# Attention and a gated feed-forward block: turning x by DMA, packing attention into the first half of the output stage, turning q in halves, and moving a set of value rims behind the weights

## The chip, the cores and the metric

The kernel runs on one core of a Trainium2 chip. The metric is the time of one execution on the device, in microseconds (us). Executions of one kernel mostly agree within a few tenths of a per cent (the kernel before: 277.99 to 278.3 us in four runs). Four engines do the work: PE (matrix products), DVE and ACT (vector and scalar work), POOL (here mostly copies and the issue of loads). SP here only issues DMA transfers (its timelines hold nothing else). In the views, PEld is the loading of PE's weights.

## The reference, cut to what matters

```python
# q, k, v: (4 batches, 8 heads, 768 positions, 64)
k_sum = k in blocks of 32 positions, maximum of each block
v_sum = v in blocks of 32 positions, mean of each block
scores = window of 16 positions on each side, and all 24 block sums (+ log 32)
attn   = softmax(scores) @ concat(v, v_sum)
x      = attn, heads side by side: (3072 tokens, 512)
out    = x + sigmoid(x @ w_res) * ((gelu(x @ w_gate) * (x @ w_val)) @ w_out)   # d_ff = 1536
```

## The kernel before: the parts that matter

The tokens are worked off in eight units of 384 (a batch is two units). Each unit has a projection stage (12 groups: a gate product `g` and a value product `vv` of four matmuls each, Gelu on ACT, their product `gvT` on DVE) and an output stage (three blocks of 128 tokens: `res_step` for the sigmoid, twelve matmuls `f` with w_out, the end on DVE). The attention of the *next* unit is woven into the output stage: per head pair scores `s` (PE), the exponential `P` (ACT), the mask (DVE), the product with v, `ao` (PE), and the normalized `xn` (DVE). The projection's matmuls are written for x with features on the partitions (`xT`), so `xn` is turned (transposed): on PE, by three transposes per feature block (0.17 us), and a copy by DVE (0.35 us).

```python
def xt_step(u, ko, st, pool, tag, copy=nc.vector.tensor_copy):
    xp = pool.tile([128, TU], BF16, tag=tag, name="xp")
    for sub in range(NSUB):
        nc.tensor.transpose(xp[:, sub * 128:(sub + 1) * 128],
                            st["xn"][:, sub, ko * 128:(ko + 1) * 128], ident[:])
    copy(st["xT"][:, ko, :], xp[:])

def mid_out(u, st, gvT, nst):              # output stages 1 to 6
    n = u + 1
    s_step(n, 0, nst)
    res_step(st, 0)
    ffn_step(st, gvT, 0, 0, FO)            # the 12 f matmuls of block 0
    av_step(n, 0, nst)
    s_step(n, 1, nst)
    end_step(u, st, 0)
    res_step(st, 1)
    ffn_step(st, gvT, 1, 0, 4)
    av_step(n, 1, nst)
    s_step(n, 2, nst)
    ffn_step(st, gvT, 1, 4, FO)
    av_step(n, 2, nst)
    s_step(n, 3, nst)
    xt_step(n, 0, nst, ps_t, "t")
    # ... av_step 3 and xt_step 1 to 3 among the f matmuls of block 2
```

The scores have one PSUM buffer (`ps_s`, bufs=1): the scores of the second head pair wait until the exponential of the first has read them. In units 3 and 5 DVE also makes the block maxima of k for the next batch (`k_blocks`, four times a reduction and a copy), after projection groups 4 to 7. The value rims (`v_rims`) are the 16 positions on each side of a window, which DMA copies from the neighbouring blocks of v.

The softmax here doesn't subtract the row's maximum and nothing guards it: scores larger than these inputs give would overflow.

## Time and profile before

The median is 278.05 us (277.99 to 278.26). PE is what bounds it. The first lines of the profile page, the kernel before (engine, busy us, share of the span, instructions), and two rows of its 40 slices (tenths of busy PE; tenths of the granted clock):

```profile
PE 262.2 (95%) x2352; PEld 142.7 (52%) x2377; DVE 161.9 (59%) x365; ACT 128.7 (47%) x204; POOL 101.2 (37%) x134
...
PE   6889989999999999999989999999899999999994
...
PEclk9999999999999999999999999999999999999999
```

The share says only that PE is busy nearly throughout. What a change can gain is read by stage. The windows view of the kernel before follows, with a window from the start of each stage to the start of the next. Columns: from and to; length; busy us of PE, PEld, DVE, ACT and POOL (instructions in brackets); granted clock; DMA share; GB/s. The six rows are output stage 0, output stage 1, projection 3, output stage 3, projection 4 and output stage 4.

```profile
41.61:56.24 14.63, 13.93 (x158) 6.87 (x158) 7.12 (x16) 8.16 (x12) 5.48 (x9) 1.00 1.42 174
76.89:90.72 13.83, 13.57 (x155) 7.05 (x158) 8.64 (x19) 7.81 (x9) 13.83 (x20) 1.00 1.41 106
122.04:140.74 18.70, 17.10 (x112) 9.42 (x110) 14.92 (x24) 5.93 (x13) 7.72 (x8) 1.00 0.24 43
140.74:154.57 13.83, 13.57 (x155) 7.05 (x158) 8.64 (x19) 7.81 (x9) 13.83 (x20) 1.00 1.68 123
154.57:170.48 15.91, 15.91 (x100) 9.29 (x98) 7.93 (x15) 5.93 (x13) 7.23 (x11) 1.00 1.65 189
170.48:184.31 13.83, 13.57 (x155) 7.04 (x158) 8.64 (x19) 7.81 (x9) 0.00 (x0) 1.00 0.09 34
```

A middle output stage takes 13.83 us every time. A plain projection stage takes 15.91 us, projection 3 takes 18.70. Its block sums (12 matmuls) explain 0.76 us; the other 2 us are mostly PE waiting for DVE (its busy time is 17.10 of the 18.70). The PE timeline of the kernel before shows the turning of x at the end of output stage 4 (start, length, instruction; a line merges several), and the waits of projection 3 in brackets, with what ended them:

```profile
136.52 0.81 PE L307 MATMUL g<-xT,w_gate 128*128 128x384 bf16 x4 [0.23 <-DVE gvT L313]
139.34 0.81 PE L307 MATMUL g<-xT,w_gate 128*128 128x384 bf16 x4 [1.37 <-DVE gvT L313]
...
183.97 0.50 PE L296 MATMUL xp<-ident,xn 128*128 128x128 bf16 x6
184.31 1.03 PE L307 MATMUL g<-xT,w_gate 128*128 128x384 bf16 x4
185.18 0.81 PE L307 MATMUL vv<-xT,w_val 128*128 128x384 bf16 x4
```

Six transposes hold PE from 183.97 to 184.31, so three cost 0.17 us and the twelve of a unit 0.68 us. The first group's `g` needs 0.87 us to the start of `vv` instead of 0.65: it waits for DVE's copies of the last two turned blocks (the second ends at 184.96, and the last matmul of `g` starts at 185.0).

The start is bound by DMA: it moves 196 to 208 GB/s in every 4 us from 24 to 44 us, PE waits 0.82 us for q until 36.15, and output stage 0 begins its f matmuls when w_out lands:

```profile
44.08 1.90 PE L339 MATMUL f<-w_out,gvT 128*128 128x512 bf16 x8 [0.29 <-DMA w_out<-in_moe_w_out_dram]
```

### The profile page before, as it was taken

The page shows a single profiled execution, that of the slowest core. Times are in us where ns is not written, and L with a number is a line of the kernel's source. Part 1 is how long each engine was busy: PE and PEld are TensorE (multiplying, and loading weights), DVE is VectorE, ACT ScalarE, POOL GpSimd, SP SyncE. Part 2 cuts the span into 40 slices and gives each one's busy share as a digit, 9 for nine tenths or more (in the row PEclk, how much of TensorE's full clock was granted, in tenths as well). Part 3 has the DMA queues.
Part 4 walks back from the last instruction along what each step waited for, and adds up shares of the span by engine and source line. Part 5 has one row for each costly group of instructions (what it writes and reads, how often), then busy time and mean ns, then how long its engine had stood idle before and what let it go on. Part 6 is the DMA issues. An engine that isn't in the chain of part 4 may idle for free.

```text
span 276.5 us, 5854 instructions
## 1 busy us (share of the span) xinstructions
PE 262.2 (95%) x2352; PEld 142.7 (52%) x2377; DVE 161.9 (59%) x365; ACT 128.7 (47%) x204; POOL 101.2 (37%) x134
## 2 busy tenths in 40 slices
PE   6889989999999999999989999999899999999994
PEld 2445644555545555446544565446444555555543
DVE  5856423598338533685947743685947743684424
ACT  1776347474565446343345336343256336343320
POOL 8795672340699932000799912000800000000000
PEclk9999999999999999999999999999999999999999
DMA  5999999999089999104099997104001100111003
GB/s 89 169 134 195 196 204 206 153 164 165 6 54 139 197 145 153 40 38 94 2 68 135 191 188 109 40 38 95 1 0 40 76 2 0 40 39 40 0 0 114
DMA packets 91274, 26.00 MB, mean 94 GB/s; under 512 B 75176, under 2 KB 88304, under 8 KB 91248
## 3 DMA queue, kind: packets, MB, share of 16 engines
q0 software_dynamic: 63664, 14.69, 57.9%
q1 hardware_dynamic: 27584, 10.96, 19.1%
q8 instruction: 18, 0.29, 0.4%
q14 instruction: 8, 0.07, 0.1%
HBM read 29.36 MB, written 6.29 MB: 129 GB/s over the span
## 4 chain that ended last, share of the span: by engine, by line
PE 75%; DMA 11%; DVE 4%; POOL 4%; issue 3%; ACT 1%; POOLq 0%; DVEq 0%
PE f L339 20%; PE g L307 19%; PE vv L307 18%; PE r L329 7%; DMA w_out<-in_moe_w_out_dram 5%; DMA w_gate<-in_moe_w_gate_dram 4%; PE ao L285 3%; PE s L267 3%; DMA q_sb<-in_q_dram 3%; PE xp L296 2%; DVE ks L199 2%; DVE gvT L313 2%; POOL vext L104 1%; PE f L360 1%; PE tp L224 1%
## 5 line engine op out<-in xcount | busy, mean ns | idle before, releaser
L313 DVE TENSOR_TENSOR gvT<-ge,vv 128x384 bf16<-128x384 f32 x96 | 52.6, 552 | 58.5 <-PE vv L307 56.4
L312 ACT ACTIVATE ge<-g 128x384 f32<-128x384 f32 x96 | 47.0, 491 | 82.7 <-DVE gvT L313 42.9
L307 PE MATMUL g<-xT,w_gate 128*128 128x384 bf16 x384 | 80.0, 326 | 2.5 <-DVE gvT L313 2.3
L307 PE MATMUL vv<-xT,w_val 128*128 128x384 bf16 x384 | 78.4, 326 | 0.3 <-DVE gvT L313 0.3
L339 PE MATMUL f<-w_out,gvT 128*128 128x512 bf16 x262 | 62.6, 379 | 1.6 <-issue 1.0
L307 PEld LDWEIGHTS <-w_val 128*128 128x128 bf16 x384 | 37.4, 98 | 26.3 <-issue 1.9
L307 PEld LDWEIGHTS <-w_gate 128*128 128x128 bf16 x384 | 35.7, 98 | 27.5 <-issue 5.8
L271 ACT ACTIVATE P<-s,bias_t 128x768 bf16<-128x768 f32 x32 | 28.9, 902 | 31.9 <-PE s L267 31.8
L257 POOL COPY vext<-vsum 32x1536 bf16<-32x1536 bf16 x14 | 20.0, 1467 | 62.9 <-DMA vsum<-vpart 62.8
L339 PEld LDWEIGHTS <-gvT 128*128 128x128 bf16 x276 | 26.1, 98 | 29.9 <-DMA w_out<-in_moe_w_out_dram 0.8
L104 POOL DMA_DIRECT2D vext<-in_v_dram x48 | 33.1, 761 | 13.3 <-DMA w_out<-in_moe_w_out_dram 5.3
L274 DVE TENSOR_TENSOR P<-P,maskt 128x768 bf16<-128x768 bf16 x32 | 17.7, 556 | 20.6 <-ACT P L271 18.9
L329 PE MATMUL r<-w_res,xT 128*128 128x512 bf16 x88 | 23.9, 381 | 0.4
L345 DVE SCALAR_TENSOR_TENSOR th<-th,f 128x512 f32<-128x512 f32 (+1 forms) x25 | 16.5, 658 | 6.1 <-PE f L339 5.8
L291 DVE TENSOR_TENSOR xn<-ao,rz 128x384 bf16<-128x384 f32 x32 | 17.8, 558 | 1.1
L347 DVE SCALAR_TENSOR_TENSOR o<-th,xn 128x512 f32<-128x512 f32 (+1 forms) x25 | 16.8, 670 | 0.9
L117 POOL DMA_DIRECT2D k_nat<-in_k_dram x24 | 16.4, 746 | 0.0
L199 DVE TENSOR_REDUCE ks<-kW 128x24 bf16<-128x768 bf16 x16 | 15.1, 943 | 1.6 <-ACT kW L214 1.4
L332 ACT ACTIVATE th<-r 128x512 f32<-128x512 f32 x24 | 14.2, 595 | 3.4 <-PE r L329 2.9
L289 DVE RECIPROCAL rz<-ao 128x6 f32<-128x6 f32 x32 | 6.1, 192 | 16.3 <-PE ao L285 16.2
L285 PEld LDWEIGHTS <-P 128*64 128x64 bf16 x384 | 8.7, 110 | 13.6 <-DVE P L274 6.4
L285 PE MATMUL ao<-vext,P 128*64 128x65 bf16 x384 | 12.1, 199 | 0.9 <-DVE vext L238 0.7
(69 smaller groups left out, 188.0 us busy)
## 6 DMA issues: line engine op xcount, KB each, us to landing
out_dram<-o SPq DMA_DIRECT2D x23, 256.0 KB
vext<-in_v_dram POOLq DMA_DIRECT2D x48, 64.0 KB, 5.8
q_sb<-in_q_dram POOLq DMA_DIRECT2D x4, 384.0 KB, 8.9
w_gate<-in_moe_w_gate_dram POOLq DMA_DIRECT2D x6, 256.0 KB, 9.8
w_val<-in_moe_w_val_dram POOLq DMA_DIRECT2D x6, 256.0 KB, 10.5
w_out<-in_moe_w_out_dram POOLq DMA_DIRECT2D x3, 512.0 KB, 14.2
k_nat<-in_k_dram POOLq DMA_DIRECT2D x24, 64.0 KB, 2.9
q_nat<-in_q_dram POOLq DMA_DIRECT2D x12, 128.0 KB, 5.0
```

The lines of the kernel that those rows point to most:

```text
L104: nc.gpsimd.dma_start(out=vext[b % 2][0:QT, t, :, 0:D], in_=v[b, :, t * QT:(t + 1) * QT, :].rearrange("h p d -> p h d"))
L199: nc.vector.tensor_reduce(out=ks.rearrange("d (t n) -> d t n", n=2), in_=kw[:, :, 0:QT].rearrange("d t (n w) -> d t n w", w=BLK), axis=myb ...
L257: eng.tensor_copy(vext[b % 2][96:128, lo:hi, :, 0:D], src)
L271: nc.scalar.activation(P.rearrange("p a t q -> p a (t q)"), s[:, :, 0:TU], AF.Exp, scale=scale, bias=bias_t[:])
L274: nc.vector.tensor_mul(Pf, Pf, maskt.unsqueeze(1).to_broadcast([128, 2 * HT, QT]))
L285: nc.tensor.matmul(ao[64 * e:64 * e + 64, sub, hh, :], P[:, hh, t, :], vext[b % 2][:, half * HT + t, 2 * hp + hh, 0:D + 1], start=True, st ...
L291: nc.vector.tensor_mul(xn, ao[:, :, :, 0:D], rz.to_broadcast([128, NSUB, 2, D]))
L307: nc.tensor.matmul(ps[:, 0:TU], w[:, ko, fo * 128:(fo + 1) * 128], st["xT"][:, ko, :], start=(ko == 0), stop=(ko == KO - 1), skip_group_ch ...
L312: nc.scalar.activation(ge[:], g[:, 0:TU], AF.Gelu)
L313: nc.vector.tensor_mul(gvT[:, fo, :], ge[:], vv[:, 0:TU])
L329: nc.tensor.matmul(r[:], st["xT"][:, ko, ss], w_res[:, ko, :], start=(ko == 0), stop=(ko == KO - 1))
L339: nc.tensor.matmul(st["f", sub][:], gvT[:, fo, ss], w_out[:, fo, :], start=(fo == 0), stop=(fo == FO - 1), skip_group_check=True)
```

## The change

The intent: PE should not turn x. A DMA that transposes does it for units 2 to 7, which takes longer, so all attention of the next unit goes into the first half of the output stage, and x has the second half to land. The last two projection groups are drawn together (gate, gate, value, value), so that Gelu ends earlier and ACT can switch to the exponential earlier (the table load of that switch takes 1.28 us). The first group uses the last quarter of x last. Loads wait behind a small POOL copy that reads the landed x (`pool_after`), so that the DMA queues are clear. q of later batches is loaded one unit later and turned in two halves; the k blocks move to groups 8 to 11 (and the block sums of units 3 and 5 from group 0 to group 1); the second set of value rims of batch 0 moves from SP at the start to the POOL queue, behind the weights of the projections and w_res and ahead of w_out. Cut to its core:

```diff
-        v_rims(0, HT, NT)                    # SP, at the start
...
         nc.gpsimd.dma_start(out=w_res[:], ...)
+        v_rims(0, HT, NT, nc.gpsimd)
         # then the three loads of w_out
...
+        def xt_dma(ko, st):
+            nc.sync.dma_start_transpose(out=st["xT"][:, ko].rearrange("d (s k) -> d s k", k=128),
+                                        in_=st["xn"][:, ko].rearrange("p s d -> p (s d)"))
...
+        def fo_first(st, gvT):               # group 0 of units 2 to 7
+            g, vv = mm_tile("g"), mm_tile("vv")
+            for kos in (range(KO - 1), (KO - 1,)):
+                gv_mm(g, w_gate, st, 0, kos)
+                gv_mm(vv, w_val, st, 0, kos)
+            gv_end(gvT, 0, g, vv)
+
+        def fo_last_two(st, gvT): ...        # g 10, g 11, vv 10, vv 11; units 1 to 7
...
         def mid_out(u, st, gvT, nst):
             s_step(n, 0, nst)
             res_step(st, 0)
-            ffn_step(st, gvT, 0, 0, FO)
+            ffn_step(st, gvT, 0, 0, 2)
+            s_step(n, 1, nst)
+            ffn_step(st, gvT, 0, 2, 6)
             av_step(n, 0, nst)
-            s_step(n, 1, nst)
+            xt_dma(0, nst)
+            s_step(n, 2, nst)
+            ffn_step(st, gvT, 0, 6, 11)
+            av_step(n, 1, nst, **other)
+            xt_dma(1, nst)
+            s_step(n, 3, nst)
+            ffn_step(st, gvT, 0, 11, FO)
+            res_step(st, 1)
+            av_step(n, 2, nst)
+            xt_dma(2, nst)
+            ffn_step(st, gvT, 1, 0, 4)
+            av_step(n, 3, nst, **other)
+            xt_dma(3, nst)
             ...                              # then the rest of the f matmuls
-            xt_step(n, 3, nst, ps_mm, "mm")
...
+                    pool_after(st["xT"][0:1, KO - 1, 0:1])    # before the k and v loads
...
-                    elif 4 <= fo < 4 + NP:
-                        k_blocks(nb, fo - 4)
+                    elif 8 <= fo < 8 + NP:
+                        k_blocks(nb, fo - 8)
```

More of the change, by code (lines that the diff above doesn't have):

```diff
@@ L72 @@
     gate1 = const.tile([1, 1], F32, name="gate1")
+    gate2 = const.tile([1, 1], BF16, name="gate2")
     kW = [const.tile([128, NT, NP, 128], BF16, name=f"kW{i}") for i in range(2)]
@@ L105, in v_loads, with v_rims, load_k_nat @@
                                 in_=v[b, :, t * QT:(t + 1) * QT, :].rearrange("h p d -> p h d"))
-    def v_rims(b, lo, hi):
+    def v_rims(b, lo, hi, eng=nc.sync):
         x = vext[b % 2]
         a, e = min(hi, NT - 1), max(lo, 1)
-        nc.sync.dma_start(out=x[QT:QT + WIN, lo:a, :, 0:D], in_=x[0:WIN, lo + 1:a + 1, :, 0:D])
-        nc.sync.dma_start(out=x[QT + WIN:BAND, e:hi, :, 0:D], in_=x[QT - WIN:QT, e - 1:hi - 1, :, 0:D])
+        eng.dma_start(out=x[QT:QT + WIN, lo:a, :, 0:D], in_=x[0:WIN, lo + 1:a + 1, :, 0:D])
+        eng.dma_start(out=x[QT + WIN:BAND, e:hi, :, 0:D], in_=x[QT - WIN:QT, e - 1:hi - 1, :, 0:D])
     k_sb, q_sb = {}, {}
-    def load_nat(b):
+    def load_k_nat(b):
         for t in range(NT):
@@ L118, in load_nat, with load_q_nat @@
                                 in_=k[b, :, t * QT:(t + 1) * QT, :].rearrange("h p d -> p h d"))
+    def load_q_nat(b):
         for c in range(NQ):
@@ L121, in load_nat, with turn_k, turn_q @@
                                 in_=q[b, :, c * 128:(c + 1) * 128, :].rearrange("h p d -> p h d"))
-    def turn_all(b):
+    def turn_k(b):
         nc.sync.dma_start_transpose(out=kW[b % 2].rearrange("d t g k -> d (t g) k")[:, :, 0:QT],
                                     in_=k_nat.rearrange("p t f -> p (t f)"))
-        nc.sync.dma_start_transpose(out=qT[b % 2].rearrange("d c g k -> d (c g) k"),
-                                    in_=q_nat.rearrange("p c f -> p (c f)"))
+    def turn_q(b, half):
+        cs = slice(half * NSUB, (half + 1) * NSUB)
+        nc.sync.dma_start_transpose(out=qT[b % 2][:, cs].rearrange("d c g k -> d (c g) k"),
+                                    in_=q_nat[:, cs].rearrange("p c f -> p (c f)"))
     with tc.manual_schedule():
@@ L289, in av_step @@
             nc.vector.reciprocal(rz[:], ao[:, :, :, D:D + 1])
-            xn = st["xn"].rearrange("p s (h d) -> p s h d", d=D)[:, :, 2 * hp:2 * hp + 2, :]
+            xn = st["xn"][:, hp].rearrange("p s (h d) -> p s h d", d=D)
             nc.vector.tensor_mul(xn, ao[:, :, :, 0:D], rz.to_broadcast([128, NSUB, 2, D]))
@@ L296, in xt_step @@
                 nc.tensor.transpose(xp[:, sub * 128:(sub + 1) * 128],
-                                    st["xn"][:, sub, ko * 128:(ko + 1) * 128], ident[:])
+                                    st["xn"][:, ko, sub, :], ident[:])
             copy(st["xT"][:, ko, :], xp[:])
+        def xt_dma(ko, st):
+            nc.sync.dma_start_transpose(out=st["xT"][:, ko].rearrange("d (s k) -> d s k", k=128),
+                                        in_=st["xn"][:, ko].rearrange("p s d -> p (s d)"))
         def new_unit():
-            return {"xn": upool.tile([128, NSUB, DM], BF16, tag="xn", name="xn"),
+            return {"xn": upool.tile([128, KO, NSUB, 128], BF16, tag="xn", name="xn"),
                     "xT": upool.tile([128, KO, TU], BF16, tag="xT", name="xT")}
@@ L323, in fo_step, with fo_last_two @@
             gv_end(gvT, fo, g, vv)
+        def fo_first(st, gvT):
[4 more added lines that the diff above has]
+            gv_end(gvT, 0, g, vv)
+        def fo_last_two(st, gvT):
+            g = [mm_tile("g"), mm_tile("g")]
+            for i in range(2):
+                gv_mm(g[i], w_gate, st, FO - 2 + i, range(KO))
+            for i in range(2):
+                vv = mm_tile("vv")
+                gv_mm(vv, w_val, st, FO - 2 + i, range(KO))
+                gv_end(gvT, FO - 2 + i, g[i], vv)
         def res_step(st, sub):
@@ L346, in end_part @@
             o = work.tile([128, n], F32, tag="o", name="o")
-            nc.vector.scalar_tensor_tensor(o[:], th[:, cs], 0.5, st["xn"][:, sub, cs], ALU.mult, ALU.add)
+            x = st["xn"][:, cs.start // 128:cs.stop // 128, sub, :]
+            nc.vector.scalar_tensor_tensor(o.rearrange("p (k d) -> p k d", d=128),
+                                           th[:, cs].rearrange("p (k d) -> p k d", d=128), 0.5, x,
+                                           ALU.mult, ALU.add)
             row = u * TU + sub * 128
@@ L474, in mid_out @@
             n = u + 1
+            other = dict(pool=ps_t, tag="t")
             s_step(n, 0, nst)
             res_step(st, 0)
-            ffn_step(st, gvT, 0, 0, FO)
+            ffn_step(st, gvT, 0, 0, 2)
+            s_step(n, 1, nst)
+            ffn_step(st, gvT, 0, 2, 6)
             av_step(n, 0, nst)
-            s_step(n, 1, nst)
+            xt_dma(0, nst)
[11 more added lines that the diff above has]
+            xt_dma(3, nst)
             end_step(u, st, 0)
-            res_step(st, 1)
-            ffn_step(st, gvT, 1, 0, 4)
-            av_step(n, 1, nst)
-            s_step(n, 2, nst)
             ffn_step(st, gvT, 1, 4, FO)
-            av_step(n, 2, nst)
-            s_step(n, 3, nst)
-            xt_step(n, 0, nst, ps_t, "t")
+            res_step(st, 2)
             end_step(u, st, 1)
-            res_step(st, 2)
-            ffn_step(st, gvT, 2, 0, 4)
-            av_step(n, 3, nst)
-            xt_step(n, 1, nst, ps_t, "t")
-            ffn_step(st, gvT, 2, 4, FO)
-            xt_step(n, 2, nst, ps_t, "t")
-            xt_step(n, 3, nst, ps_mm, "mm")
+            ffn_step(st, gvT, 2, 0, FO)
             end_step(u, st, 2)
@@ L505, in last_out, with pool_after @@
             last_step(u, st, gvT, NSUB - 1)
+        def pool_after(x):
+            nc.gpsimd.tensor_copy(gate2[:], x)
         for u in range(NU):
@@ L509 @@
             nb = b + 1
-            if half == 0 and nb < B:
-                if nb == 1:
-                    k_sb[nb] = load_qk(k, nb, 1, "k_sb")
-                    v_loads(nb)
-                    for i in range(2):
-                        q_sb[2 * nb + i] = load_q(nb, i)
-                else:
-                    load_nat(nb)
-                    v_loads(nb)
+            if half == 0 and nb == 1:
+                k_sb[nb] = load_qk(k, nb, 1, "k_sb")
+                v_loads(nb)
+                for i in range(2):
+                    q_sb[2 * nb + i] = load_q(nb, i)
             if u:
@@ L521 @@
             for fo in range(0 if u else 2, FO):
-                fo_step(st, gvT, fo)
+                if u > 1 and fo == 0:
+                    fo_first(st, gvT)
+                elif u and fo == FO - 2:
+                    fo_last_two(st, gvT)
+                elif u == 0 or fo < FO - 2:
+                    fo_step(st, gvT, fo)
                 if u == 0 and fo >= 8:
@@ L526 @@
                     q_step(1, 1, fo, ps_t, "t")
+                if half == 0 and 1 < nb < B and fo == 0:
+                    pool_after(st["xT"][0:1, KO - 1, 0:1])
+                    load_k_nat(nb)
+                    v_loads(nb)
+                if half == 0 and b and fo == 1:
+                    v_rims(b, HT, NT)
                 if half == 0 and 1 < nb < B and fo == 6:
-                    turn_all(nb)
+                    turn_k(nb)
                     k_rims(nb, slice(0, NP), nc.gpsimd)
@@ L531 @@
                     if fo == 0:
-                        v_rims(nb, 0, NT)
-                    if fo == (4 if nb == 1 else 0):
+                        v_rims(nb, 0, HT)
+                        if nb > 1:
+                            pool_after(st["xT"][0:1, KO - 1, 0:1])
+                            load_q_nat(nb)
+                    if fo == (4 if nb == 1 else 1):
                         vsum_grp(nb, ps_t, "t")
@@ L536 @@
                             vsum_bc(nb, 3 * i, 3 * i + 3, nc.gpsimd)
+                        if nb > 1:
+                            turn_q(nb, 0)
+                            turn_q(nb, 1)
                     if nb == 1:
```

## The prediction

> **What bounds the kernel now.** TensorE. The page gives PE 262.2 of 276.5 us busy (95%), the clock row is full throughout, and the chain of waits is 75% PE. Cut by stage (windows table, PE timeline), a middle output stage takes 13.83 us, and the projection stage after it 15.91 us (units 4, 6, 7), of which 24 groups of 0.65 us are 15.6; its first group takes 0.87 us. Units 3 and 5 take 18.70 and 18.55 us: 0.76 is the block-sum matmuls, and about 2.0 is the k-block maxima (0.94 us each, their copy up to 1.48 us while POOL copies) holding DVE, so that PE waits for gvT. The load stage (0 to 44 us) is bound by DMA: PE loses about 1.0 us before the q turn at 36.15 and 0.29 us for w_out at 44.08.
>
> **What changes.** Six of the seven PE turnings of x go: 12 transposes are about 0.68 us of PE per unit, with four DVE copies (1.4 us, off the path). The first projection group's loss (0.22 us) goes too, if the x that DMA turns is there in time. Added: about two more switches between f and attention matmuls per stage. From the trace's pieces (s 0.28, ao 0.31, r 0.87, f 0.217 each plus about 0.09 per switch) I estimate the new output stage at 13.25 us. Gain per unit 0.58 + 0.22 = 0.8 us; times six, 4.7 us.
>
> **Will packing stall?** By the trace's durations (exp 0.90, tanh 0.59, mask 0.56, rz + xn 0.8), with Gelu of the last two groups pulled forward, exp and mask just keep ahead of s and ao, with 0.1 to 0.5 us to spare. The last x is written about 9.1 us into the stage and needed at about 14.3. The turn of q (24 blocks) was issued in 4.54 us and DMA traffic ended about 1.8 us later; three blocks should take, as an estimate, 2.5 to 3.5 us, against 5.2 us available. [...] the trace's k loads land in 2.5 to 2.9 us. The loads gated behind x keep the queues clear.
>
> **k blocks.** Moved to groups 8 to 11, they now queue before the first mask on DVE. I expect PE to lose about 1.85 us at the first ao of units 3 and 5 instead of 2.0 in the projection: a move, hardly a gain. The halves of q should land 1 us or more before their s.
>
> **Start.** The second rims leave a moment when DMA is not full (17 to 19 us) and join the weights' queue, ahead of w_out. q should land earlier, w_out no earlier, perhaps 1 us later: net 0, give or take 0.8.
>
> **Sum.** 278.05 - 4.7 - 0.3 = 273.0 us, range 270.5 to 275.5. Chances: faster by over 2% 0.38, within 2% 0.60, slower 0.02.
>
> **What would show it.** Right: no xp after unit 1; middle output stages at 13.1 to 13.4 us; first projection group without a wait; units 3 and 5 with a wait for DVE at the first ao; w_out's wait at the first output stage grown, the q wait shrunk. DVE busy about 8 us less.
>
> **What would make it wrong.** x landing later than 5 us after its multiply (DMA transposes slower than estimated, or queued behind the turn of k or q): every unit would wait in its first group, and 2 us each would eat all. Exp being late for the single score buffer: 0.5 us per step. A w_out later by more than 1 us. On the good side: matmul switches costing nothing (0.3 us per stage), or k blocks hidden wholly (4 us in all), which would pass 2%.

The estimate of 2.5 to 3.5 us for x to land: of what stands behind it, the trace before shows the turn of q (24 blocks issued in 4.54 us, DMA traffic over about 1.8 us later; three twenty-fourths of the one and the whole of the other make 2.4 us; the other turn of q was issued in 8.38 us) and the k loads (2.5 us at the least, 2.9 in the median, 5.1 at the most). DMA "not full" is 85 and 163 GB/s in the two microseconds from 17 to 19 there, against 195 from 30 to 31.

## More of the kernel before

In unit 1, PE turns q after groups 7 to 10 (`q_step`), and ACT copies it out.

## The result, and the profile after

The changed kernel takes 275.35 us (275.06 to 276.2, 4 runs), the kernel before 278.15 us in the same rounds. The ratio is 0.9904 (95% interval 0.9882 to 0.9927). A ratio is the mean time of one kernel's runs over that of the other's of the same rounds, so not quite the ratio of the medians quoted. The gain is 2.8 us; 5.0 was the centre of the prediction. The time lies in the predicted range (270.5 to 275.5), by 0.15 us.

The page after, the same lines as shown of before:

```profile
PE 257.3 (94%) x2280; PEld 138.6 (51%) x2305; DVE 155.3 (57%) x341; ACT 128.6 (47%) x204; POOL 103.4 (38%) x140
...
PE   7889988999989999999979999999989999999994
```

The windows view of the changed kernel, the same six stages in the same order:

```profile
41.53:57.09 15.56, 13.97 (x157) 6.94 (x157) 7.12 (x16) 8.15 (x12) 6.69 (x10) 1.00 1.46 175
77.64:92.08 14.44, 13.07 (x146) 6.39 (x146) 8.17 (x17) 8.28 (x10) 2.53 (x5) 1.00 0.23 64
122.62:139.18 16.56, 16.56 (x109) 9.44 (x108) 10.15 (x17) 6.57 (x13) 8.22 (x9) 1.00 1.28 124
139.18:154.13 14.95, 13.07 (x143) 6.29 (x145) 11.66 (x23) 7.16 (x9) 3.50 (x5) 1.00 0.23 63
154.13:169.82 15.69, 15.69 (x97) 9.29 (x95) 7.38 (x13) 6.56 (x13) 15.24 (x23) 1.00 1.60 133
169.82:183.09 13.27, 13.01 (x143) 6.30 (x145) 8.36 (x18) 7.17 (x9) 2.58 (x5) 1.00 1.23 127
```

Undisturbed, the idea works as costed: output stage 4 takes 13.27 us (estimate 13.25) and the projection after it loses 0.22 us. But output stages 0, 1 and 3 became *longer*: 15.56, 14.44 and 14.95 us. PE is busy for only 13.07 of the 14.95. The PE timeline of the changed kernel names the three new waits:

```profile
44.93 1.90 PE L365 MATMUL f<-w_out,gvT 128*128 128x512 bf16 x8 [1.01 <-DMA w_out<-in_moe_w_out_dram]
...
80.49 0.35 PE L273 MATMUL s<-qT,kW 64*128 64x64 bf16 x12 [1.10 <-ACT P L277]
...
143.80 0.38 PE L291 MATMUL ao<-vext,P 128*64 128x65 bf16 x12 [1.61 <-DVE P L280]
```

Unit 5 has a wait like the last one too (1.04 us at 204.10, and 0.24 us for gvT before it). Summed over all stages of the two traces (spans 276.5 and 273.5 us):

| part | predicted, us | measured, us |
|---|---|---|
| x by DMA, six output stages and first groups at the undisturbed 0.57 + 0.22 | -4.7 | -4.7 |
| k blocks: projections and output stages 3 and 5, beyond that | -0.3 | -0.3 |
| output stage 1 beyond that: s waits for the exponential | 0 | +1.2 |
| start, up to the end of output stage 0 | 0 | +0.85 |
| sum | -5.0 | -3.0 |

Was x in time? Yes. The view by tile gives the DMA transposes of the changed kernel (duration is the issue on SP, in ns; then us from issue to landing, minimum, median, maximum):

```profile
L307 SPq DMA_TRANSPOSE xT<-xn x24: 1177/1203/2284, 83.2 to 239.1; - x24
...
DMA to landing us min/median/max: 2.3/3.0/4.1
```

The POOL copy that waits for the last block ran at 90.2 us for unit 2, whose first matmul on that block was at 93.05: 2.8 us to spare. Of the 3.0 us to landing, SP spent 1.2 us (median) on the issue.

### The profile page after: what moved, and what is told of

It is laid out like the page before. It is cut to its first block, busy times and chain, and to the rows that moved or that the text cites. A ratio compares the mean times of both kernels' runs of the same rounds, so it can differ in the third digit from the quotient of the medians.

```text
span 273.5 us, 5780 instructions
## 1 busy us (share of the span) xinstructions
PE 257.3 (94%) x2280; PEld 138.6 (51%) x2305; DVE 155.3 (57%) x341; ACT 128.6 (47%) x204; POOL 103.4 (38%) x140
## 4 chain that ended last, share of the span: by engine, by line
PE 74%; DMA 11%; DVE 5%; POOL 4%; issue 3%; ACT 1%; POOLq 0%; DVEq 0%
PE f L365 20%; PE g L317 20%; PE vv L317 19%; PE r L355 6%; DMA w_out<-in_moe_w_out_dram 4%; DMA w_val<-in_moe_w_val_dram 4%; PE ao L291 3%; DMA q_sb<-in_q_dram 3%; PE s L273 2%; DVE ks L205 2%; POOL vext L105 1%; DVE gvT L323 1%; POOL w_gate L182 1%; PE f L389 1%; PE tp L230 1%
## 5 line engine op out<-in xcount | busy, mean ns | idle before, releaser
L317 PE MATMUL g<-xT,w_gate 128*128 128x384 bf16 x384 | 78.6, 326 | 0.1
L365 PE MATMUL f<-w_out,gvT 128*128 128x512 bf16 x262 | 64.8, 380 | 1.4 <-DMA w_out<-in_moe_w_out_dram 1.0
L365 PEld LDWEIGHTS <-gvT 128*128 128x128 bf16 x276 | 24.8, 98 | 28.2 <-DMA w_out<-in_moe_w_out_dram 1.5
L355 PEld LDWEIGHTS <-xT 128*128 128x128 bf16 x96 | 8.8, 98 | 9.2
```

The costliest lines, as they stand in the source:

```text
L317: nc.tensor.matmul(ps[:, 0:TU], w[:, ko, fo * 128:(fo + 1) * 128], st["xT"][:, ko, :], start=(ko == 0), stop=(ko == KO - 1), skip_group_ch ...
L355: nc.tensor.matmul(r[:], st["xT"][:, ko, ss], w_res[:, ko, :], start=(ko == 0), stop=(ko == KO - 1))
L365: nc.tensor.matmul(st["f", sub][:], gvT[:, fo, ss], w_out[:, fo, :], start=(fo == 0), stop=(fo == FO - 1), skip_group_check=True)
```

## The experiments

There were twelve runs in three calls. The kernels of one call ran on one chip (experiments 1 to 4 on one, all others on another) and share the runs of the kernel before (278.03, 277.86 and 277.86 us).

### 1. Rims back at the start

```diff
         v_rims(0, 0, HT)
+        v_rims(0, HT, NT)
...
-        v_rims(0, HT, NT, nc.gpsimd)
```

> Undoes one part: the second set of value rims goes back to the sync queue at the start. My theory: the rims cost 0.86 us because they sit in the weights' queue ahead of w_out; so PE waits about 0.3 us for w_out instead of 1.0 (first output stage starts its f at about 44.1 us instead of 44.9), and the kernel takes 274.5 us (0.85 less than 275.35). The rival, that the late w_out has another cause (the run of the start merely differs): no change, 275.3 us, f still at 44.9. The q turn stays at 36.1 us under both.

Measured: 276.40 us, ratio 0.9945 (0.9914 to 0.9975). It did not get faster; the expectation of 274.5 us was missed. In its trace the wait for w_out did shrink, to 0.31 us, but the whole stream of weights came later: q landed so that its turn began at 37.35 us instead of 36.14, and f began at 45.35, later than 44.93. So a shorter wait in one place is no gain in time.

### 2. Two empty transfers in place of the rims

```diff
         v_rims(0, 0, HT)
+        v_rims(0, HT, NT)
...
-        v_rims(0, HT, NT, nc.gpsimd)
+        for i in range(2):
+            nc.gpsimd.dma_start(out=dum[:, 32 * i:32 * i + 32], in_=warm[0:1, 0:32])
```

> Rims back on the sync queue, but two empty transfers of 64 bytes stand in their place ahead of w_out. If the rims cost time because they push w_out two places back in the POOL queue (the issue of w_out moved from 30.4 to 33.0 us), w_out lands as late as after the change: f at 44.9 us, 275.3 us in all. If it is the rims' own data (some 1,400 pieces of 128 bytes) that is served before w_out, f is back at about 44.1 us and the time at 274.5 us.

Measured: 276.56 us, ratio 0.9936 (0.9916 to 0.9957). f began at 45.34 us, with 0.51 us of wait for w_res and 0.68 for w_out. That lies between the two predictions for the wait, and the start as a whole was as late as in run 1. It does not tell the two apart.

### 3. q of unit 1 turned one group earlier

```diff
-                        elif 7 <= fo < 7 + NP:
-                            q_step(nb, 0, fo - 7, ps_t, "t")
+                        elif 6 <= fo < 6 + NP:
+                            q_step(nb, 0, fo - 6, ps_t, "t")
```

> In unit 1 the four PE turnings of q come one projection group earlier (groups 6 to 9 instead of 7 to 10), so that the last is no longer queued behind the two last groups drawn together. My theory: its copy on ACT (77.75 us) held back the table load for Exp and so the second score group; the 1.10 us wait of s for the exponential in unit 1 goes, that output stage shrinks from 14.44 to about 13.3 us, and the kernel takes 274.2 us. Rival: the wait comes from the packed order itself (only two f matmuls between the first two score groups); then it stays, and the time is 275.3 us.

In the changed kernel, the ACT timeline around output stage 1 was this:

```profile
76.15 0.49 ACT L322 ACTIVATE ge<-g 128x384 f32<-128x384 f32 x1 [0.16 <-PE g L317]
77.75 0.48 ACT L232 COPY qT<-tp 128x384 bf16<-128x384 bf16 x1 [1.11 <-PE tp L230]
78.25 1.28 ACT L277 ACT_TABLE_LOAD   x1
79.54 0.90 ACT L277 ACTIVATE P<-s,bias_t 128x768 bf16<-128x768 f32 x1
```

Gelu is done at 76.64, but the copy of q stands between it and the table load. In program order, the last turn of q follows group 10, and the change put group 11 inside group 10. So it now comes after all of the projection, and ACT idles 1.11 us for it. With q one group earlier, output stage 1 took this (windows view of run 3):

```profile
79.07:92.34 13.27, 13.27 (x146) 6.29 (x146) 8.37 (x18) 7.17 (x9) 2.17 (x4) 1.00 0.26 70
```

It takes 13.27 us and PE never idles, so the theory holds and the rival (the packed order itself) falls. The timed runs hide it: 275.93 us, from 274.14 to 278.15, ratio 0.9922 (0.9883 to 0.9961). The fastest, 274.14, is what was expected. The profiled run was the slowest of the six, and its trace shows why: a spell of half clock. The windows view of run 3, 1 us each after a first of 2 us (the granted clock is the third number from the right):

```profile
144.00:146.00 2.00, 0.94 (x26) 0.71 (x27) 1.92 (x6) 0.24 (x1) 0.00 (x0) 1.00 0.00 0
146.00:147.00 1.00, 1.00 (x7) 0.24 (x6) 0.58 (x2) 0.66 (x1) 0.00 (x0) 0.82 0.00 0
147.00:148.00 1.00, 1.00 (x26) 0.83 (x26) 0.68 (x3) 0.03 (x1) 0.00 (x0) 0.50 0.02 8
148.00:149.00 1.00, 1.00 (x3) 0.30 (x2) 0.42 (x2) 0.87 (x1) 0.00 (x0) 0.50 0.55 115
149.00:150.00 1.00, 1.00 (x3) 0.15 (x1) 0.46 (x1) 0.00 (x0) 0.00 (x0) 0.50 0.45 89
150.00:151.00 1.00, 1.00 (x16) 0.58 (x16) 0.44 (x2) 0.60 (x1) 0.00 (x0) 0.97 0.06 10
```

This came after PE had waited 2.27 us at the first ao of unit 3 (until 145.06), and cost that stage about 1.5 us more: 17.10 us, where run 2's trace, with the same wait of 2.27 us but at full clock, has 15.61. The granted clock was 0.50 in the three full slices, and with 0.82 and 0.97 on either side the spell lasted about 3.4 us, an estimate from these slices. What starts such a spell in one execution and not in the next was not shown.

### 4. k blocks spread over groups 2, 4, 6 and 8

```diff
-                    elif 8 <= fo < 8 + NP:
-                        k_blocks(nb, fo - 8)
+                    elif fo in (2, 4, 6, 8):
+                        k_blocks(nb, fo // 2 - 1)
```

> The k block maxima of units 3 and 5 come at projection groups 2, 4, 6, 8 instead of 8 to 11. My theory: PE's waits at the first ao (1.61 and 1.04 us) and for gvT (0.24 us) come from DVE working off four block maxima just before the first mask; spread out, each fits into the 0.75 us that DVE idles per group. Output stages 3 and 5 fall from 14.95 and 14.38 to about 13.3 us, projection stages 3 and 5 to about 16.45; time 272.1 us (3.2 less). Rival: the wait is the block-sum copies on POOL [...]; then the ao waits stay, and the time stays within 0.5 us of 275.35.

The DVE timeline of the changed kernel, just before the wait of 1.61 us in unit 3 (`ks` is the maximum over blocks, `kW<-ks` its copy, `P<-P,maskt` the mask):

```profile
138.63 1.46 DVE L209 COPY kW<-ks 128x288 bf16<-128x288 bf16 x1
140.01 1.00 DVE L323 TENSOR_TENSOR gvT<-ge,vv 128x384 bf16<-128x384 f32 x2
140.94 0.94 DVE L205 TENSOR_REDUCE ks<-kW 128x24 bf16<-128x768 bf16 x1
141.91 0.23 DVE L209 COPY kW<-ks 128x288 bf16<-128x288 bf16 x1
142.06 0.94 DVE L205 TENSOR_REDUCE ks<-kW 128x24 bf16<-128x768 bf16 x1
143.04 0.23 DVE L209 COPY kW<-ks 128x288 bf16<-128x288 bf16 x1
143.19 1.02 DVE L280 TENSOR_TENSOR P<-P,maskt 128x768 bf16<-128x768 bf16 x2
```

DVE never idles here; the mask that ao waits for is simply last in line. The same copy takes 0.23 us alone and 1.46 us at 138.63, while POOL makes its copies of the block sums (1.47 us each, 135.7 to 141.4); the POOL timeline of the changed kernel has them in one line:

```profile
135.72 5.70 POOL L263 COPY vext<-vsum 32x1536 bf16<-32x1536 bf16 x4 [8.34 <-DMA vsum<-vpart]
```

The stretched copy ends at 140.09 us, about when the POOL copy that began at 138.54 does (140.00). DVE's other work beside POOL's copies is not stretched: the reduction keeps its 0.94 us (at 137.66), the product `gvT` its 0.54 us (at 137.20). Why only the copy is, was not shown. Its stretch of 1.23 us is most of the wait of 1.61 us. In the six traces with the blocks in groups 8 to 11, the copies of a unit took 1.05 to 2.40 us more than the 0.23 us each that they take alone, and PE's loss (the wait at the first ao, and what the projection took over 16.56 us) was 0.24 to 0.28 us more than that in all twelve units. So without POOL's copies, by this estimate, about 0.3 us of the 1.61 would be left. Spread out, projection 3, output stage 3, projection 5 and output stage 5 took (windows view of run 4):

```profile
122.68:139.25 16.57, 16.57 (x111) 9.44 (x109) 12.23 (x22) 6.59 (x13) 8.04 (x9) 1.00 1.31 124
139.25:152.51 13.26, 13.26 (x145) 6.29 (x145) 8.88 (x18) 7.16 (x9) 3.08 (x5) 1.00 0.25 67
181.47:198.03 16.56, 16.56 (x109) 9.43 (x108) 12.38 (x22) 6.59 (x13) 9.39 (x10) 1.00 1.20 126
198.03:211.30 13.27, 13.27 (x146) 6.29 (x146) 8.37 (x18) 7.17 (x9) 0.95 (x1) 1.00 0.25 68
```

PE is busy for the whole of all four stages. They sum to 59.66 us; in the changed kernel they took 16.56 + 14.95 + 16.96 + 14.38 = 62.85 us. That is 3.2 us less, as expected. The time is 273.77 us (272.29 to 274.18), ratio 0.9837 (0.9814 to 0.9859); 272.1 was expected, and only the fastest run came near it. But this run does not separate the theory from the rival that blames POOL: POOL's copies still run at the same time (from 135.76 us in unit 3), yet the spread also moved three of the four blocks out of their way, and the copies of a unit lost only 0.1 and 0.25 us. The trace of run 6 (below), with the same spread, does separate them. There POOL's copies in unit 5 met two of DVE's again (DVE timeline of run 6):

```profile
191.96 1.28 DVE L209 COPY kW<-ks 128x288 bf16<-128x288 bf16 x1
195.06 1.00 DVE L209 COPY kW<-ks 128x288 bf16<-128x288 bf16 x1
```

The first ao waited all the same for nothing, and output stage 5 took 13.26 us; the projection paid about 0.5 us (17.03 against 16.56). So both belong to the cause: beside POOL's copies DVE's took up to 1.28 us here (1.46 us in the changed kernel) instead of 0.23, and the lump just before the mask leaves DVE no idle time to make it up.

### 5. The changed kernel again

> The changed kernel itself, on the chip and in the rounds of the next three, since the first four experiments showed that single runs spread by 1 to 3 us (the start of the weights' stream and dips of the granted clock). Expected ratio to the kernel before 0.990, like its first measurement; the stages after the start as in the first trace, the start itself (first f of the first output stage) anywhere from 44.5 to 46 us.

Measured: 276.27 us, ratio 0.9948 (0.9924 to 0.9971), so only 1.6 us faster than before on this chip. This misses the expected 0.990. Its profiled run waited 1.85 us at the first ao of unit 3, with no half clock after it, and 1.71 us at that of unit 5, after which the clock was at 0.50 for 3.4 us; output stage 5 took 16.52 us.

### 6 and 7. Both repairs together, and with the rims back at the start

Run 6 joins the edits of experiments 3 and 4; run 7 adds that of experiment 1.

> The two repairs that held in their stages (q turned one group earlier in unit 1, block maxima spread over groups 2, 4, 6, 8 in units 3 and 5), rims left behind the weights. If they add: 1.1 + 3.0 us less than the changed kernel, ratio to before about 0.975, fastest runs near 271 us. The rival, that a saved wait comes back later as another (x or exp late instead), would leave it at 0.983 like the spread block maxima alone.

> As the run before, but the second rims back on the sync queue at the start. Two theories of the start: (a) the rims cost the same wherever they stand, since the weights' stream is full from about 18 us on and carries the same bytes: same time as the run before, within 0.4 us, with less wait for w_out and more for q and w_val. (b) Standing before w_out costs 0.7 to 0.9 us: this run is that much faster. The first single-part run spoke for (a), the traces' w_out waits (0.31 against 1.01 us) for (b).

(The "full" stream was 187 GB/s from 20 to 24 us and 196 to 197 GB/s from 24 to 36 us in the trace of run 6.)

Measured: run 6 took 272.06 us (271.55 to 272.46), ratio 0.9788 (0.9776 to 0.9801); run 7 took 271.69 us (271.22 to 272.14), ratio 0.9776 (0.9762 to 0.979). The repairs nearly add: 276.27 - 272.06 = 4.2 us less than the changed kernel on the same chip, and output stages 1, 3 and 5 last 13.26 to 13.27 us in both traces. (The ratio of 0.975 was missed, since the changed kernel itself was at 0.9948 here.) Against run 4 alone, the earlier q turn is also seen in the timed runs: 0.9788 against 0.9837, with intervals apart. Projection 5 took 17.03 and 17.26 us in these two traces, not 16.56: a part of the wait comes back there, as experiment 4 explains. Between the two places of the rims lie 0.4 us, with overlapping intervals, and run 7's profiled run had half clock at its start (from 21.5 us, for 3.4 us). That is nearer to theory (a), that the rims cost the same at either place, but four runs each do not exclude (b). Run 7 has the lowest median of all versions; runs 6 and 10 are not told apart from it.

### 8. x turned by PE again, in the packed order

```diff
-            xt_dma(0, nst)
             s_step(n, 2, nst)
             ffn_step(st, gvT, 0, 6, 11)
             av_step(n, 1, nst, **other)
-            xt_dma(1, nst)
+            xt_step(n, 0, nst, ps_o, "ao")
...                                            # and likewise blocks 1 to 3, one step later
```

> The changed kernel with one part undone: x of units 2 to 7 turned by PE again (12 transposes and four copies by DVE per unit), everything else, the packed order too, as in the change. My theory: turning by DMA is worth the PE time of the transposes, 0.7 us per output stage, so this takes 4 us more than the changed kernel, about 279.5 us, above the kernel before; packing saves nothing itself. Rival: packing hides waits that the old order had; then it lies between, at 277 us or less.

Measured: 281.35 us (280.41 to 282.2), ratio 1.0114 (1.0096 to 1.0131), 5.1 us above the changed kernel of the same rounds. The undisturbed output stages 2 and 4 last 14.04 us against 13.27: 0.77 us each. The windows view of run 8, output stage 4:

```profile
174.44:188.48 14.04, 14.04 (x157) 7.05 (x157) 9.34 (x22) 7.16 (x9) 4.09 (x6) 1.00 0.78 74
```

So the DMA turning is the gain (six times 0.77 is 4.6 us), and the changed kernel without it, with its waits in units 1, 3 and 5 and at the start, is 3.5 us slower than the kernel before. The rival falls. The stages are the safer measure here: four of the five timed runs had a mean clock of 0.994 or less. The profiled run also had a late start: the first rims landed late (2.58 us of wait at the first ao, until 22.98 us), and half clock began during that wait and lasted from 21.1 to 27.9 us.

### 9. The kernel before again

> The kernel before itself, for a second trace of its start on a chip that also runs the changed versions. If the first output stage's late f (44.9 to 45.3 us in nearly all traces of changed versions, 44.1 in the one trace of before) is due to the change, f starts at about 44.1 us again and the time from the q turn to f is about 7.9 us; if it is the run or the chip, f starts at 44.9 us or later here too. Ratio 1.000 either way.

Measured: ratio 1.0015 (0.9997 to 1.0034). f began at 44.07 us, with no wait for w_out. Together with the first trace, before is twice at 44.1.

### 10. Best version without the gate on the loads

Here both `pool_after(...)` calls are taken out of the version of run 7.

> Base of this run and the next two: the version with all three repairs (271.7 us). Here the POOL copies that hold the k, v and q loads until x has landed are taken out, so the k and v loads run in output stages 1 and 3, beside the DMA turning of x, as the loads did in the kernel before. In the changed kernel x lands about 2.8 us before it is needed (gate copy at 90.2 us, its first matmul at 93.05). My theory: crowded queues bring x from 3 to some 5 us, still in time: no wait in the first groups, time within 0.4 us of 271.7. Rival (the change's intent): x comes over 3 us later, PE waits 1 us or more at the start of units 2 and 4, 273.5 us or more.

Measured: 272.31 us, ratio 0.9803 (0.9779 to 0.9826). x landed after 4.8 us in the median instead of 3.0, and no first group waited. The two runs at full clock took 271.57 and 271.68 us; the other two, at a mean clock of 0.98, took 272.94 and 273.5. So the median missed the expected 0.4 us around 271.7, and the runs at full clock met it. With the loads beside it the turning is slower, by 1.8 us in the median, but within the time it has, and no need for the gate was shown.

### 11. Best version with the last two groups plain

```diff
-                elif u and fo == FO - 2:
+                elif False:
                     fo_last_two(st, gvT)
-                elif u == 0 or fo < FO - 2:
+                else:
                     fo_step(st, gvT, fo)
```

> The last two projection groups plain again (gate, value, gate, value) instead of gate, gate, value, value. My theory: Gelu of the last group and so the Exp table load come 0.6 us later, the second score group of each middle output stage waits about 0.55 us for the first exponential: stages of 13.8 us instead of 13.26, 3.3 us in all, 275.0 us. Rival: there is slack and it costs under 0.5 us in all.

Measured: 274.78 us, ratio 0.9892 (0.9867 to 0.9917). The PE timeline of run 11 in output stage 4 shows the wait, the same 0.46 us in five of the six stages:

```profile
169.14 0.59 PE L365 MATMUL f<-w_out,gvT 128*128 128x512 bf16 x2
170.19 0.35 PE L273 MATMUL s<-qT,kW 64*128 64x64 bf16 x12 [0.46 <-ACT P L277]
```

Those stages last 13.79 or 13.80 us. So drawing the two groups together is a needed part of packing, worth about 3 us.

### 12. Best version with x by DMA in the old order

The output stage is that of the kernel before, with `xt_dma` right after each `av_step`.

> x turned by DMA, but the output stage in the order of the kernel before (ao spread over the whole stage). My theory: packing is there only to give DMA its time. The last xn is then ready about 0.3 us before the stage ends, x lands 3 us later, and the first projection group of units 2 to 7 waits about 2 us each: 12 us in all, 284 us, and such waits may bring spells of half clock on top. Rival: the projection group's split (last quarter of x used last) hides most of it: under 275 us.

Measured: 279.19 us, ratio 1.0041 (1.0018 to 1.0065), 7.5 us more than run 7. The PE timeline of run 12, first group of unit 6:

```profile
216.70 0.65 PE L317 MATMUL vv<-xT,w_val 128*128 128x384 bf16 x3
218.31 0.32 PE L317 MATMUL g<-xT,w_gate 128*128 128x384 bf16 x1 [0.96 <-DMA xT<-xn]
```

The waits are 0.96 to 1.40 us in units 2 to 7 (6.5 us in all), about half of what was expected, in part because x landed 2.3 us after its issue in the median, not 3. The theory holds, its size was too large: without packing, DMA turning ends slower than the kernel before.

## Why the prediction was right or wrong

**The turning of x (right, to the tenth).** "Gain per unit 0.58 + 0.22 = 0.8 us" was measured as 0.57 + 0.22. x landed in 3.0 us in the median (estimate 2.5 to 3.5; the longest took 4.1). Runs 8 and 12 show that neither half of the idea does it alone.

**The k blocks (right).** They were called "a move, hardly a gain": the two projections lost 2.14 and 1.45 us, and the output stages gave back 1.12 and 0.55 instead of gaining 0.57 each. Net of the part that is x, that is 0.3 us. The wait at the first ao, forecast at 1.85 us, was 1.61 and 1.04 us. What the prediction named only as a hope ("k blocks hidden wholly", 4 us) was a matter of four numbers in the program: run 4 gained 3.2 us of it.

**"Exp and mask just keep ahead" (wrong for unit 1).** The margins were worked out for a plain unit, and hold there: five of the six output stages do not wait for the exponential. Unit 1 has q turns among its groups, and drawing groups 10 and 11 together moved the last of them behind the whole projection, so that its copy on ACT delayed the table load. Cost: 1.2 us. Run 3 took it away.

**"Start ... net 0, give or take 0.8" (mis-sized).** The term measured +0.85 us in the two traces. The predicted signs ("w_out's wait grown, the q wait shrunk") came half true: w_out's wait was 1.0 to 1.4 us in five traces with the rims late, and 0 to 0.64 in four with the rims early (runs 7 and 8, whose start had half clock, are left out here and below, and run 2 with its empty transfers here); the q wait in the first trace after was 0.81 us, as good as unchanged. But the place of the rims does not settle the time: f began at 44.9 to 45.0 (and once 46.3) with the rims late, and at 44.25 to 45.35 with the rims early. Why the kernel before was at 44.1 twice is open.

**What was not foreseen: half clock.** A mean clock of 0.994 over 275 us is what one spell of about 3.4 us at 0.5 leaves, as an estimate. Taking a mean of 0.994 or less as the sign, such spells were in 1 of 32 runs of before, in 14 of 33 runs of versions with the long wait at the first ao in units 3 and 5, and in 8 of 25 runs of the others. So the wait is not the only occasion. Two spells seen in traces began 1.6 and 0.6 us after such a wait (of 2.27 and 1.71 us), and two more (runs 7 and 8) at the end of or during a wait for the first rims, but six other waits of 1.5 to 2.3 us, in five traces, had none. Why the changed versions have more of them is open. They explain a part of why the repeat gained only 1.6 us and not the 3.0 us of the first two traces: its three runs at a mean clock of 0.998 or more took 275.25 to 276.02 us, which is 1.8 to 2.6 us less than before.

**The overall.** The time fell into the range at its upper edge, and the verdict "within 2%" was the likelier one predicted. The centre was 2.35 us too low, and unit 1 and the start account for 2.0 of it. That the time lay inside the range, by 0.15 us, is partly luck: the repeat (276.27 us, on a chip where before took 277.86) lay outside. One listed sign also failed in size: DVE's busy time fell by 6.6 us, where about 8 was listed.

## What to carry to other kernels

Before drawing two steps of a loop together, look at what else stands between them in any iteration: the gain came in the plain units, and the loss in the one unit that had extra work there. When side work is moved off one engine's critical stretch, spread it over stretches where that engine idles a little each time (here DVE, 0.75 us per projection group); put in one lump before the next deadline it only moves the wait, and whatever stretches it there (here POOL's copies, beside which a copy of 0.23 us took 1.46) adds to the wait in full. Check the granted clock after a long wait: here it was at 0.50 for about 3.4 us after two of eight such waits (1.71 and 2.27 us), though that the wait caused it was not shown. A slow but free engine such as DMA (here 3.0 us to land a block) can replace a fast busy one (0.17 us of PE for its three transposes), if the order of work is rebuilt to give it its time.
